# Three edits in the start-up of a fused Sinkhorn attention and expert-layer kernel: order of a sort step, width of warm-up matmuls, parts of a weight load

## The chip, the cores and the metric

One core of a Trainium2 chip runs the whole kernel. The metric is the device time of one execution in microseconds, the median of three runs. The core has five engines that run their own instruction queues and meet at semaphores: TensorE (PE; its weight loads are shown as PEld), VectorE (DVE), ScalarE (ACT), GpSimd (POOL) and SyncE (SP). Transfers are issued from the queues of GpSimd (those that change the type from f32 to f16) and SyncE, and are carried out by 16 DMA engines.

## The reference

Two parts follow each other. The attention part has q, k and v of shape (4 batches, 8 heads, 768 tokens, 64) and an 8 x 8 matrix `sort_net` for each batch and head; the expert part has 3072 tokens of width 512, four experts, and hidden width 1024:

```python
P = sort_net
for _ in range(5):
    P = np.exp(P - np.max(P, axis=-1, keepdims=True))
    P = P / (np.sum(P, axis=-1, keepdims=True) + 1e-09)
    P = P / (np.sum(P, axis=-2, keepdims=True) + 1e-09)
k_sorted = np.einsum('bhij,bhjcd->bhicd', P, k_b)   # 8 blocks of 96 tokens are mixed
v_sorted = np.einsum('bhij,bhjcd->bhicd', P, v_b)
# each block of 96 queries attends to its own block of sorted keys and values
...
p = domain_probs / (domain_probs.sum(-1, keepdims=True) + 1e-09)
for e in range(E):
    out += p[:, e:e + 1] * (np.maximum(x @ w1[e], 0.0) @ w2[e])
```

The scores are scaled by 1/8 and normalized by a softmax over the 96 keys of the block.

## The kernel before

All order is written out by hand: each engine executes its instructions in the order of the program text, and the tile framework adds the semaphore waits. Matrix operands are f16, sums are f32 in PSUM. PSUM is split into two rings of two buffers each: `psM` (taken by `psm`) and `psA` (taken by `psa`). A buffer is written again only when its readers are done.

Batch 0 is treated apart, since everything waits for it at the start. Its stages are:

- Loads. SyncE issues `sort_net` and the expert weights' probabilities. GpSimd issues, in this order, the first half of the queries (two transfers), k and v of the first four heads ("quad 0"), k and v of quad 1, and expert 0's first matrix `w1sb[0]` in two transfers (`load_w1(0, 2)`, line 173): rows 0 to 255 of the 512 (chunks `kc` 0 and 1 of 128 rows), then rows 256 to 511, each with all 1024 columns. Then it builds masks, an identity and constants.
- Warm-up. `warm(84)` (line 280) issues 84 matmuls of a constant 128 x 128 tile `dummy` with itself; their result is not used. In the last of the five sort iterations two calls of `h_q` transpose the queries on TensorE, and `warm(30)` (line 288) follows.
- Sort iterations. Five rounds of exp (ScalarE), two sums, two reciprocals and two products (VectorE) on 32 x 64 values. The last product, repeated over 16 columns into f16 (`sn16`, line 304), is split: VectorE makes rows 0 to 3 of the 8, GpSimd rows 4 to 7.
- Transposing the sort matrices. `r_half(a)` transposes one half of `sn16` with four matmuls into `Rv[:, a]`, which lies in one `psM` buffer (`ps_R`). `r_half(0)` runs at once; VectorE builds `PI0[0]` from it, the mixing operands of the lower four blocks.
- Mixing and attention. `mix_half(nm, qd, hf, pool)` mixes k or v of a quad into half `hf` of the sorted blocks with 24 matmuls, of 64 columns each; `mixed` copies two or four of the blocks out of PSUM. `h_s` makes scores with 8 matmuls and takes their exp on ScalarE; `h_w` transposes the sorted values and copies them out; `h_a` multiplies scores with values; `h_x` transposes the result into `xTs[0]`, the input of the experts.
- Expert 0's first layer, interleaved with the rest of the attention: `group0(qq, nq, g, kcs)` multiplies four chunks of 128 columns of `w1sb[0]` (group `g`: columns 0 to 511 or 512 to 1023) by the tokens, for the row chunks `kcs`. The first two calls, `group0(0, 1, 0, [0, 1])` and `group0(0, 1, 1, [0, 1])`, read rows 0 to 255, the next two rows 256 to 511.

In the order around the change, TensorE does `mix_half("k", 0, 0)`, `mix_half("v", 0, 0)`, `h_s(0, 0)`, `r_half(1)`, the transposes of `h_w`, `mix_half("k", 1, 0)`, `h_a(0, 0)`. VectorE copies both halves of `Rv` into `Rs` (f16, line 1372) after `r_half(1)`; `mix_half("k", 1, 0)` takes the `psM` buffer of `ps_R`, and so waits for that copy. `Rs` is read by GpSimd, for `PI0[1]` and for the operands of later batches. After that copy GpSimd issues the second half of the queries and expert 0's second matrix (`load_w2(0, 2)`).

Behind this start the kernel is a long row of matmuls: the experts' two layers for twelve groups of 256 tokens, most of them by a seven-product (Strassen-like) scheme, with the attention of batches 1 to 3 interleaved by the lists `PLANS`.

Of the kernel before, what the change touches and what calls it, by code (L numbers as in the profile page):

```python
# [17 lines left out]
def kernel(  # L18
# [11 lines left out]
    nc = tc.nc  # L30
# [8 lines left out]
    P = 128  # L39
# [10 lines left out]
    KH = NFC // 2  # L50
# [16 lines left out]
    def psa(shape, dtype, name):  # L67
        state["n"] += 1
        return psA.tile(shape, dtype, tag="ps", name=name)
# [36 lines left out]
    def load_natural(b, nm, qd):  # L106
        src = {"k": k, "v": v}[nm]
        t = arena[:, ds(("k", "v").index(nm) * 2 * NW + qd * NW, NW)].rearrange("p (h r d) -> p h r d", h=4, r=R)
        natural[(b, nm, qd)] = t
        nc.gpsimd.dma_start(  # L110
            t.rearrange("p h r d -> p h (r d)"),
            src[b, ds(4 * qd, 4)].rearrange("h (p r) d -> p h (r d)", r=R),
        )
# [12 lines left out]
    w1sb, w2sb = [], []  # L126
# [4 lines left out]
    def load_w1(e, parts=1):  # L131
        n = NKC // parts
        for i in range(parts):
            nc.gpsimd.dma_start(
                w1sb[e][:, ds(i * n, n)], moe_w1[e].rearrange("(kc p) f -> p kc f", p=P)[:, ds(i * n, n)]
            )
# [8 lines left out]
    def load_half_queries(hf):  # L145
        for qd in range(2):
            nc.gpsimd.dma_start(
                q0[ds(64 * qd, 64), hf].rearrange("p h r d -> p h (r d)"), half_queries(qd, hf)
            )

    dummy = Hflat[:, ds(2 * NFC * 2 * P, P)]
# [18 lines left out]
    load_natural(0, "v", 0)  # L170
    load_natural(0, "k", 1)
    load_natural(0, "v", 1)
    load_w1(0, 2)

    eye16 = const.tile([P, CP], F16, name="eye16")
    maskk = const.tile([P, P], F16, name="maskk")
# [52 lines left out]
    def spread_weights():  # L229

        nc.vector.tensor_reduce(p_den, p_in, AX.X, ALU.add)
        yield
        nc.vector.tensor_scalar(out=p_den, in0=p_den, scalar1=1e-9, scalar2=None, op0=ALU.add)
        yield
        nc.vector.reciprocal(p_den, p_den)
        yield
        nc.vector.tensor_tensor(
            p_out.rearrange("p e t -> p t e"), p_in, p_den.broadcast_to([P, NT, E]), ALU.mult
        )
        p_rows = p_dram.rearrange("e (p t) -> p e t", t=NT)  # L240
        nc.sync.dma_start(p_rows[0:S_P], p_out[0:S_P])
        nc.sync.dma_start(p_0, p_dram[0, 0:S].rearrange("(t p) -> t p", p=P))
        pbs[(0, 0)] = load_p(0, 0)
        nc.sync.dma_start(p_rows[S_P:P], p_out[S_P:P])
        yield
# [10 lines left out]
    def warm(n):  # L256
        ps = psM.tile([P, 4, P], F32, tag="ps", name=f"ps_w_{state['n']}")
        state["n"] += 1
        for m in range(n):
            nc.tensor.matmul(ps[:, m % 4, :], dummy, dummy, start=True, stop=True)  # L260

    qT0 = [from_spare(2 * S).rearrange("p (s f r x) -> p s f r x", s=2, f=2, r=R) for _ in range(2)]

    def h_q(qd, hf, copy):

        ps = psa([P, 2, R, 64], F16, f"ps_q_{qd}_{hf}")
        rows = ds(64 * qd, 64)
        for sg in range(2):
            for r in range(R):
                for hh in range(2):  # L270
                    nc.tensor.transpose(
                        ps[ds(D * hh, D), sg, r, :], q0[rows, hf, 2 * sg + hh, r, :], ident[rows, rows]
                    )
        copy(qT0[qd][:, :, hf], ps[:])
# [2 lines left out]
    srow = const.tile([GH, NB, 1], F32, name="srow")  # L277
    scol = const.tile([GH, NB, 1], F32, name="scol")
    sn16 = const.tile([GH, NB, NB, CP], F16, name="sn16")
    warm(84)  # L280
    p_steps = spread_weights()
    nc.gpsimd.tensor_copy(ident6, ident[0:R, 0:R])
    for it in range(5):
        nc.scalar.activation(sn[:], sn[:], AF.Exp, bias=0.0, scale=1.0)
        if it == 4:
            for qd in range(2):
                h_q(qd, 0, nc.scalar.copy)
            warm(30)
        nc.vector.tensor_reduce(srow[:], sn[:], AX.X, ALU.add)
        nc.vector.reciprocal(srow[:], srow[:])  # L290
        nc.vector.tensor_tensor(sn[:], sn[:], srow[:].broadcast_to([GH, NB, NB]), ALU.mult)
        nc.vector.tensor_reduce(scol[:], sn[:].rearrange("p i j -> p j i"), AX.X, ALU.add)
        nc.vector.reciprocal(scol[:], scol[:])
        if it < 4:
            nc.vector.tensor_tensor(
                sn[:], sn[:],
                scol[:].rearrange("p j o -> p o j").broadcast_to([GH, NB, NB]),
                ALU.mult,
            )
            if it:  # L300
                next(p_steps)
# [10 lines left out]
    Rv = ps_R[:, :, 0:HB * GH].rearrange("p a (i g) -> p a i g", g=GH)  # L312

    def r_half(a):
        for i in range(HB):
            nc.tensor.matmul(
                Rv[:, a, i, :], sn16[:, a * HB + i, :, :].rearrange("g j c -> g (j c)"),
                ident[0:GH, 0:GH], start=True, stop=True,
            )
# [4 lines left out]
    Rs = const.tile([P, GH, NB], F16, name="Rs")  # L324
# [31 lines left out]
    vec, act = nc.vector.tensor_copy, nc.scalar.copy  # L356
# [128 lines left out]
    def mix_half(nm, qd, hf, pool, warm_up=0):  # L485

        ps = pool([P, 1024], F32, f"ps_m{nm}_{qd}_{hf}")
        keep_warm(ps[:, 0:P], warm_up)
        tails[(nm, qd, hf)] = ps[:, 2 * R * 64:1024].bitcast(F16).rearrange("p (n x) -> p n x", n=2)
        ps = ps[:, 0:2 * R * 64].rearrange("p (s r x) -> p s r x", s=2, r=R)  # L490
        for sg in range(2):
            for r in range(R):
                for hh in range(2):
                    h = 4 * qd + 2 * sg + hh
                    nc.tensor.matmul(  # L495
                        ps[ds(D * hh, D), sg, r, :],
                        head(0, nm, h)[:, r, :],
                        PI0[hf][:, h, :, :].rearrange("p i c -> p (i c)"),
                        start=True, stop=True,
                    )  # L500
        return ps

    def mixed(nm, qd, ps, i0, n, copy):

        dst = kTs[qd][:, 0:S] if nm == "k" else vT0[qd]
        copy(
            dst.rearrange("p (i x c) -> p x i c", i=HB, c=CP)[:, :, ds(i0, n)],
            ps.rearrange("p s r (i c) -> p (s r) i c", c=CP)[:, :, ds(i0, n)],
        )
# [30 lines left out]
    def h_s(qd, qq, ps=None):  # L540

        kT, ET = kTs[qd], ETs[2 * qd + qq % 2]
        if ps is None:
            ps = psa([P, 2, 512], F32, f"ps_s0_{qd}_{qq}")
        for n in range(4):
            for hh in range(2):
                sg, i = n // 2, 2 * (qq % 2) + n % 2

                m = BLK if 2 * i + sg == 3 else P
                nc.tensor.matmul(  # L550
                    ps[0:m, hh, ds(n * BLK, BLK)],
                    kT[ds(D * hh, D), ds((2 * i + sg) * BLK, m)],
                    qT0[qd][ds(D * hh, D), sg, qq // 2, :, ds((2 * (qq % 2) + n % 2) * CP, CP)],
                    start=True, stop=True,
                )
        nc.scalar.activation(
            ET[:, 0:S].rearrange("c (h x) -> c h x", h=2), ps[0:BLK, :, 0:HS],
            AF.Exp, bias=0.0, scale=SCALE,
        )
# [806 lines left out]
    mixed("k", 0, mk0, 0, 2, act)  # L1366
    mv0 = mix_half("v", 0, 0, psa)
    mixed("v", 0, mv0, 0, 2, vec)
    h_s(0, 0)
    r_half(1)  # L1370
    mixed("k", 0, mk0, 2, 2, act)
    vec(Rs.rearrange("p g (a i) -> p a g i", a=2), Rv.rearrange("p a i g -> p a g i"))
    load_half_queries(1)
    load_w2(0, 2)
    build_PI0(nc.gpsimd, 1, 0, H, Rs[:, 0:H, HB:NB])
# [160 lines left out]
```

## Time and profile before

| What | Value |
|---|---|
| Time, median of 3 runs | 359.16 us (359.14 to 359.62) |
| Profiled execution: span from first to last instruction | 357.8 us (its time around the span is not listed apart) |
| Instructions | 9498, of them 3949 matmuls and 3949 weight loads |
| TensorE busy | 351.6 us, 98% of the span |
| VectorE, ScalarE, GpSimd busy | 276.2, 170.6, 133.6 us |
| Granted TensorE clock | 1.00 in all slices |
| DMA share in the first 40 us | above 0.9 of the engines from about 3 us on |

In the rows of the timeline a line reads: start in us, duration in us of the merged group, engine, source line, operation, names written and read, shapes, count, and in brackets the idle time of the engine just before and what ended it; "issue" there means that the profile shows nothing that the engine waited for. In the table of windows each engine's entry is its busy time in the window and, in brackets, the number of its instructions. A matmul's duration includes its way through the array, so that matmuls issued 0.03 us apart show 0.2 us each and overlap.

### The profile page before, as it was taken

The page shows a single profiled execution, that of the slowest core. Times are in us where ns is not written, and L with a number is a line of the kernel's source. Part 1 is how long each engine was busy: PE and PEld are TensorE (multiplying, and loading weights), DVE is VectorE, ACT ScalarE, POOL GpSimd, SP SyncE. Part 2 cuts the span into 40 slices and gives each one's busy share as a digit, 9 for nine tenths or more (in the row PEclk, how much of TensorE's full clock was granted, in tenths as well). Part 3 has the DMA queues.
Part 4 walks back from the last instruction along what each step waited for, and adds up shares of the span by engine and source line. Part 5 has one row for each costly group of instructions (what it writes and reads, how often), then busy time and mean ns, then how long its engine had stood idle before and what let it go on. Part 6 is the DMA issues. An engine that isn't in the chain of part 4 may idle for free.

```text
span 357.8 us, 9498 instructions
## 1 busy us (share of the span) xinstructions
PE 351.6 (98%) x3949; PEld 306.3 (86%) x3949; DVE 276.2 (77%) x552; ACT 170.6 (48%) x303; POOL 133.6 (37%) x149
## 2 busy tenths in 40 slices
PE   8899999999999999999999999999999999999996
PEld 8686867888888888888899988888888888888886
DVE  5754797869889587868978988896678886588963
ACT  2554240442434535367947258830288611688201
POOL 8864010375122222000535318840058800188400
PEclk9999999999999999999999999999999999999999
DMA  8999999999999999935996420005200015100011
GB/s 114 207 205 228 216 210 198 209 163 165 201 154 160 188 152 170 194 74 73 168 201 90 102 78 0 2 2 108 102 29 2 3 39 138 61 0 2 2 73 46
DMA packets 72022, 40.51 MB, mean 113 GB/s; under 512 B 40614, under 2 KB 66732, under 8 KB 71980
## 3 DMA queue, kind: packets, MB, share of 16 engines
q0 software_dynamic: 36576, 19.93, 41.9%
q1 hardware_dynamic: 35260, 19.92, 28.5%
q8 instruction: 31, 0.51, 0.6%
q14 instruction: 11, 0.09, 0.1%
q10 hardware_dynamic: 144, 0.07, 0.1%
HBM read 42.13 MB, written 6.34 MB: 135 GB/s over the span
## 4 chain that ended last, share of the span: by engine, by line
PE 95%; DVE 2%; ACT 1%; DMA 0%; issue 0%; DVEq 0%
PE ps_h L790 18%; PE ps_Q L1264 18%; PE ps_p L774 12%; PE ps_X L1121 10%; PE ps_Z L1121 7%; PE ps_Q L1121 7%; PE ps_Z L1264 6%; PE ps_h L679 3%; PE ps_o L714 3%; PE ps_p L830 3%; PE ps_a L453 2%; PE ps_s L418 2%; PE ps_k L399 1%; PE ps_v L365 1%; PE ps_a L567 1%; PE ps_mk L495 1%
## 5 line engine op out<-in xcount | busy, mean ns | idle before, releaser
L790 PE MATMUL ps_h<-xT,w 128*128 128x256 f16 x576 | 67.5, 273 | 0.0
L790 PEld LDWEIGHTS <-w 128*128 128x128 f16 x576 | 55.2, 98 | 7.2
L796 DVE SCALAR_TENSOR_TENSOR Hb<-ps_h,pb 128x1024 f16<-128x1024 f32 x34 | 41.5, 1223 | 17.2 <-PE ps_h L790 15.8
L1121 PEld LDWEIGHTS <-w 128*128 128x128 f16 x480 | 43.6, 98 | 4.8
L1134 POOL TENSOR_TENSOR arena<-tmp,pb 128x512 f16<-128x512 f32 x12 | 15.2, 1275 | 65.7 <-PE ps_Z L1121 49.8
L1264 PEld LDWEIGHTS <-Hb 128*128 128x128 f16 x320 | 31.1, 98 | 3.5
L1133 ACT ACTIVATE tmp<-tmp 128x512 f32<-128x512 f32 x46 | 29.0, 632 | 3.9 <-DVE tmp L1171 3.9
L1264 PEld LDWEIGHTS <-Sb 128*128 128x128 f16 x304 | 28.3, 98 | 3.0
L1121 PEld LDWEIGHTS <-arena 128*128 128x128 f16 x312 | 27.7, 98 | 2.9
L425 ACT ACTIVATE ET<-ps_s 96x768 f16<-96x768 f32 x24 | 18.0, 802 | 25.1 <-PE ps_s L418 24.8
L121 POOL DMA_DIRECT2D arena<-in_q_dram x24 | 19.9, 838 | 25.5 <-DMA q_ring<-arena 25.2
L408 ACT CAST kT<-ps_k 64x384 f16<-64x384 f32 x48 | 22.7, 473 | 13.3 <-PE ps_k L399 12.3
L1121 PE MATMUL ps_X<-ET,arena 128*128 128x256 f16 x168 | 25.2, 272 | 0.0
L1264 PE MATMUL ps_Q<-w,Hb 128*128 128x256 f16 x192 | 24.6, 273 | 0.0
L774 PEld LDWEIGHTS <-Hb 128*128 128x128 f16 x232 | 21.8, 98 | 3.0
L1127 DVE SCALAR_TENSOR_TENSOR Hb<-ps_X,pb 128x512 f16<-128x512 f32 x27 | 18.7, 691 | 7.0 <-PE ps_X L1121 7.0
L1141 ACT COPY ps_X<-ps_Z 128x512 f32<-128x512 f32 x27 | 15.4, 571 | 17.8 <-PE ps_Z L1121 17.8
L1121 PE MATMUL ps_Z<-xT,w 128*128 128x256 f16 (+1 forms) x176 | 22.5, 258 | 0.0
L760 DVE TENSOR_TENSOR Sb<-Hb 128x512 f16<-128x512 f16 x33 | 20.6, 647 | 0.0
L1148 ACT COPY tmp<-ps_X 128x512 f32<-128x512 f32 x26 | 15.2, 585 | 9.2 <-PE ps_X L1121 6.6
L1127 DVE SCALAR_TENSOR_TENSOR Hb<-ps_Z,pb 128x512 f16<-128x512 f32 x27 | 18.4, 682 | 1.3 <-PE ps_Z L1121 1.3
L1171 DVE TENSOR_TENSOR tmp<-ps_Q,tmp 128x512 f32<-128x512 f32 x26 | 17.8, 683 | 0.8 <-PE ps_Q L1121 0.8
(266 smaller groups left out, 741.6 us busy)
## 6 DMA issues: line engine op xcount, KB each, us to landing
w<-in_moe_w_dram POOLq DMA_DIRECT2D x6, 1024.0 KB, 27.9
pb<-p_dram SPq DMA_DIRECT2D x9, 512.0 KB, 7.0
arena<-in_k_dram POOLq DMA_DIRECT2D x8, 384.0 KB, 9.3
arena<-in_v_dram POOLq DMA_DIRECT2D x8, 384.0 KB, 7.5
vs<-arena SPq DMA_DIRECT2D x36, 66.0 KB, 4.9
arena<-in_q_dram POOLq DMA_DIRECT2D x24, 96.0 KB, 7.5
out_dram<-ob SPq DMA_DIRECT2D x9, 256.0 KB, 2.0
w<-in_moe_w_dram POOLq DMA_DIRECT2D x4, 512.0 KB, 12.5
```

What stands on the lines that cost most here:

```text
L121: nc.gpsimd.dma_start(t[:, h // 2, :, h % 2, :], q[b, h].rearrange("(t p) d -> p t d", p=P))
L408: nc.scalar.copy(kT[ds(D * hh, D), r], pk[ds(D * r, D), hh].rearrange("p a (i c) -> p a i c", c=CP),)
L425: nc.scalar.activation(ETs[2 * (pr % 2) + hh][:, 0:S].rearrange("c (a x) -> c a x", a=2), pss[hh][0:BLK, :, 0:HS], AF.Exp, bias=0.0, scale ...
L760: tt(sm[0], blk(0, 1), blk(1, 1), ALU.add)
L774: nc.tensor.matmul(ps, lhs(e, f), Ts[e][rhs][:, f, :], start=(first and e == es[0] and f == 0), stop=(done and e == es[-1] and f == KH - 1 ...
L790: nc.tensor.matmul(ps[:, f, :], w1sb[e][:, kc, ds((4 * g + f) * P, P)], xT[:, kc, ds(2 * c * P, 2 * P)], start=(kc == 0), stop=(kc == NKC ...
L796: nc.vector.scalar_tensor_tensor(out=Hb[:, homes.get(e, e), ds(4 * g, 4), :], in0=ps[:], scalar=0.0, op0=ALU.max, in1=weights(e).broadcast ...
L1121: nc.tensor.matmul(dst[:, ds(f * cols, cols)], a[lhs][:, k, ds((f0 + f) * P, P)], t[rhs][:, k, :], start=(first and f == 0 and k == 0), st ...
L1127: nc.vector.scalar_tensor_tensor(out=home(i, j), in0=src.rearrange("p (f x) -> p f x", f=m), scalar=0.0, op0=ALU.max, in1=weight(j).broadc ...
L1133: nc.scalar.activation(src, src, AF.Relu, bias=0.0, scale=1.0)
L1171: tt(t12, Q, u2, ALU.add)
L1264: nc.tensor.matmul(ps, lhs(e, f), Ts[e][rhs][:, f, part], start=(first and e == 0 and f == 0), stop=(e == E - 1 and f == KH - 1), skip_gro ...
```

## The change

Three edits:

1. `load_w1(0, 2)` is replaced by four transfers: rows 0 to 255 with columns 0 to 511, the same rows with columns 512 to 1023, then rows 256 to 511 in the same two halves. Each moves half of what one transfer moved before.
2. `warm(n)` issues matmuls whose moving operand is `dummy` repeated four times, 512 columns into a whole PSUM bank, in place of 128 columns. The calls go from `warm(84)` to `warm(21)` and from `warm(30)` to `warm(8)`.
3. `r_half(1)` and the copy of `Rv` into `Rs` move ahead of `h_s(0, 0)`; the copy is made by ScalarE (`act`) and no longer by VectorE (`vec`).

```diff
-    load_w1(0, 2)
+    for i in range(2):
+        for j in range(2):
+            nc.gpsimd.dma_start(
+                w1sb[0][:, ds(2 * i, 2), ds(KH * P * j, KH * P)],
+                moe_w1[0].rearrange("(kc p) f -> p kc f", p=P)[:, ds(2 * i, 2), ds(KH * P * j, KH * P)],
+            )
...
         for m in range(n):
-            nc.tensor.matmul(ps[:, m % 4, :], dummy, dummy, start=True, stop=True)
+            nc.tensor.matmul(
+                ps[:], dummy, dummy.rearrange("p (o x) -> p o x", o=1).broadcast_to([P, 4, P]), start=True, stop=True
+            )
...
-    warm(84)
+    warm(21)
...
-            warm(30)
+            warm(8)
...
     mixed("v", 0, mv0, 0, 2, vec)
+    r_half(1)
+    act(Rs.rearrange("p g (a i) -> p a g i", a=2), Rv.rearrange("p a i g -> p a g i"))
     h_s(0, 0)
-    r_half(1)
     mixed("k", 0, mk0, 2, 2, act)
-    vec(Rs.rearrange("p g (a i) -> p a g i", a=2), Rv.rearrange("p a i g -> p a g i"))
     load_half_queries(1)
     load_w2(0, 2)
     build_PI0(nc.gpsimd, 1, 0, H, Rs[:, 0:H, HB:NB])
```

`KH * P` is 512. In the text below, `mix "k",1` stands for `mix_half("k", 1, 0)`.

## The prediction

> **What bounds the kernel now.** I read the page's shares first, then the chain that ended last, then the first 37 us by windows, then TensorE's timeline there, and last the DMA answers for single packets.
>
> ```profile
> PE 351.6 (98%) x3949; PEld 306.3 (86%) x3949; DVE 276.2 (77%) x552; ACT 170.6 (48%) x303; POOL 133.6 (37%) x149
> ...
> q8 instruction: 31, 0.51, 0.6%
> ...
> PE 95%; DVE 2%; ACT 1%; DMA 0%; issue 0%; DVEq 0%
> ```
>
> TensorE is the bound: 351.6 us busy of a 357.8 us span, 95% of the chain. What is left is the start. The windows (PE, PEld, DVE, ACT, POOL busy, clock, DMA) show where:
>
> ```profile
> 11.70:14.00 2.30, 1.97 (x61) 1.65 (x62) 1.16 (x4) 0.48 (x1) 2.30 (x4) 1.00 1.31 206
> 14.00:17.00 3.00, 2.67 (x75) 2.24 (x76) 2.29 (x6) 2.19 (x5) 3.00 (x4) 1.00 1.14 212
> 17.00:20.50 3.50, 3.09 (x69) 2.64 (x62) 2.47 (x7) 2.27 (x4) 2.18 (x5) 1.00 1.18 205
> 20.50:37.00 16.50, 16.50 (x296) 11.94 (x293) 8.35 (x17) 8.49 (x12) 8.98 (x10) 1.00 1.18 221
> ```
>
> From 20.5 us on TensorE never stops (16.50 of 16.50), so a head start won before 20.5 us goes through to the end. Before 11.79 us the sort iterations on VectorE and ScalarE set the time; the change does not touch them. Everything is decided between 11.79 and 20.5 us, a chain of hops between TensorE, ScalarE and VectorE. Its rows on TensorE:
>
> ```profile
> 1.06 7.20 PE L260 MATMUL ps_w<-Hb 128*128 128x128 f16 x84 [1.06 <-DVE Hb L152]
> 8.19 0.85 PE L271 MATMUL ps_q<-ident,T 64*64 64x64 f16 x48
> 8.97 1.85 PE L260 MATMUL ps_w<-Hb 128*128 128x128 f16 x30
> 11.79 0.26 PE L316 MATMUL ps_R<-ident,sn 32*128 32x32 f16 x4 [0.98 <-DVE sn L304]
> ...
> 13.78 0.21 PE L550 MATMUL ps_s<-Sb,kT 64*128 64x96 f16 x1 [0.19 <-ACT kT L506]
> 14.17 0.33 PE L550 MATMUL ps_s<-Sb,kT 64*128 64x96 f16 x7 [0.18 <-issue]
> 14.44 0.26 PE L316 MATMUL ps_R<-ident,sn 32*128 32x32 f16 x4
> 14.62 0.42 PE L522 MATMUL ps_mv<-ident,Sb 128*96 128x128 f16 x4
> 15.21 0.57 PE L495 MATMUL ps_mk<-Sb,arena 128*64 128x64 f16 x24 [0.16 <-DVE Rs L1372]
> ...
> 20.27 0.37 PE L522 MATMUL ps_s<-ident,Sb 128*96 128x128 f16 x3 [0.20 <-issue]
> ```
>
> Two of these stops wait for nothing in the program ("issue"): after the first matmul of h_s(0,0), and after the first transpose at 19.85. Counting matmuls and their weight loads in the timeline, they are exactly 256 instructions apart, and the page's queue q8 moved 31 packets of 16 KB for 2 x 3949 = 7898 TensorE instructions, 255 each. So the stops are ends of instruction blocks. A DMA window of 0.02 us holds one such packet:
>
> ```profile
> q8 instruction: 1, 0.02, 295.3%
> ```
>
> 295.3% of 16 engines for 0.02 us is 0.94 us: the packet lies at 11.79 to 12.73, and the stop ends 1.44 us later. The next lies at 17.86 to 18.80, and its stop ends 1.47 us later, at 20.27. Each packet starts 3.6 to 3.7 us after the stop before it ends. A block thus comes 3.65 + 0.95 + 1.45 = 6.05 us after it is asked for, and between 8 and 20 us TensorE's short matmuls eat 256 instructions about that fast. The start is partly bound by instruction fetch.
>
> **Warm-up matmuls (84 to 21, 30 to 8).** Same columns (84 x 128 = 21 x 512), 32 x 128 in place of 30 x 128. The old ones pace at 5.0 us / 47 = 106 ns until 6 us and 2.2 / 40 = 55 ns after; 128x512 matmuls elsewhere (L714, four in 1.04 us at 379 ns each) are 0.22 us apart. So 21 wide ones take about 5.0 + 9.3 x 0.22 = 7.05 us against 7.20, and 8 take 8 x 0.22 + 0.16 = 1.9 against 1.85: no time, under the sort iterations, which release TensorE at 11.79 either way. If that cover (0.98 us) were gone they would still cost within 0.1. What counts is that 85 matmuls and 85 weight loads are gone: block ends move 170 instructions later in the work. The stop at 14.17 costs 14.17 - 13.78, less one 0.02 us step, 0.37 us; the stop at 20.27 costs 0.20 on TensorE but only about 0.05 beyond what VectorE allows there (its xsl op ends at 20.32, and the next matmuls wait for it).
>
> The Trainium skill's page "Runtime: NRT & Kernel Launch", section "Instruction fetch mechanics", has the same 16 KiB blocks of 256 instructions but calls the cost of crossing "one DMA tail-bump, mostly hidden". By that rule this edit would bring nothing; these two rows say 0.37 and 0.20, and the rows decide.
>
> The Trainium skill's page "TensorE: Matmul & The Clock Gate", Part 1, speaks against fewer, idler warm-ups: an idle window of about 3.4 us halves the clock. The idle stretch before 11.79 stays near one microsecond, so by that rule nothing happens.
>
> **r_half(1) and the copy of Rs.** r_half(1) is four matmuls 0.03 us apart. It moves into the 0.19 us hole in which TensorE waits for ScalarE's kT copy (13.25 + 0.48): 0 to 0.1 us on the path, I take 0. Its input from GpSimd ends at 12.65, 12.9 with the later issues below, before 13.6. The copy costs VectorE 0.42 now; on ScalarE, where 384 columns take 0.48 and 768 take 0.81, 256 columns make about 0.37, at 13.9 to 14.3, inside ScalarE's 0.81 us of idle time before its exp. Behind that wait stand the exp and the second kT copy, neither later than now. If the cover were gone it would cost its 0.37.
>
> Step by step, before to after: h_s(0,0) finishes at 14.12 and not 14.50 (its twin at 16.45 takes 0.34 without a stop). The exp runs 14.25 to 15.05, before to 15.35. The transposes of h_w at 14.62 wait only for VectorE's copy (13.63 + 0.56 = 14.19): 14.24, gain 0.38. VectorE's evacuation (15.15) follows: 14.77, gain 0.38. mix "k",1 no longer waits for Rs: 14.62 and not 15.21, gain 0.59, but its readers are not first in line. The second transposes wait for VectorE's next copy (ends 16.04, then 15.66): gain 0.38. That is carried through 16.72, 17.34, 17.95 and 18.95; the vanished second stop adds 0.05. Sum: 0.43 us ahead at 20.5.
>
> **Expert 0's first matrix in four.** GpSimd issues four transfers of about 0.73 us where it issued two (1.43): 1.45 more, of which 1.22 lie in its idle time before L304. Its half of the sort matrices, the queries and w2 behind it are issued some 0.23 us later. The trace shows that an issue waits for the landing of the eighth one before it (w2's at 21.46 right after w1's second half landed at 6.97 + 14.2 = 21.2), so some later issues wait up to 1.7 us for quarters; the queue holds over 10 us of work then, so it does not run dry. Rows become 1 KB packets: windows of those run at 206 GB/s against 211 with 2 KB, 0.1 us on 1 MB. Benefit: the two halves landed at 18.05 and 21.2 and are first read at 19.16 and 21.67. With the 0.43 us head start the second would be read at 21.24, with nothing to spare; as quarters the rows needed there land near 20. So this part gains nothing by itself and keeps the rest. Bounds: 0.3 lost, 0.1 gained; I take 0. Later transfers keep 1.3 us or more (the weights pb land at 38.3, read at 39.6).
>
> **Sum.** The profiled span is 357.8; the median of the runs, 359.16, is 1.3 us more, lying around the span and unchanged. 359.16 - 0.43 = 358.73; I take off little for the fetch (below): 358.8. A measurement of this kernel tells about 0.2%, 0.7 us, from no change.
>
> **Rivals.**
> 1. The fetch wait moves instead of going (slower than forecast, to slower than before). In the new stream the block ends fall at instruction 13 of mix "k",0, in h_x(0,[0]) (now 17.22, then 16.85), and in work now at 24.7 and 30.2. The block needed at 16.85 is asked for when the sequencer passes the first of these. TensorE waits from 10.7 to 11.79 with that point 37 instructions ahead. If the sequencer runs that far ahead, it asks by 10.5 or earlier, and the block is there by 16.6; if it runs only some 25 ahead, as the packet at 11.79 taken back 3.65 us suggests, it asks at 12.0, the block comes at 18.05, and 1.2 us are lost: 0.8 slower, 359.9. For running far ahead: the packet at 198.60 starts 1.67 us, 31 instructions, before TensorE gets to its block end, with its own delay still to be added. A smaller form: 256 instructions between 24.7 and 30.2 take 5.5 us, below the 6.05, so 0 to 0.4 may be lost there. It decides from a request later than 10.8 us. Place: 359.2 to 360.1. Chance 0.23.
> 2. More comes than the sum: the 0.59 of mix "k",1 and both stops in full (0.59 + 0.20) go through, because ScalarE's kT copies and not VectorE's were last: 358.3, range 358.0 to 358.5. Against it: VectorE's rows follow each other without a gap from 15.15. Chance 0.19.
> 3. The change does not do what it says: stops are a fixed price per block end and land elsewhere on the path, leaving only Rs: about 0.1 to 0.2, 359.0. Against it: block ends at 26.8 and 33.1 show no stop. Chance 0.10.
>
> The forecast itself (358.4 to 359.1) has 0.48.
>
> **Numbers.** Faster by over 0.2% (under 358.44): rival 2 nearly whole (0.17) and the forecast's edge (0.07), 0.24. Slower (over 359.88): 0.15, the upper part of rival 1 with a DMA wait taken in. Within: 0.61. The range 358.1 to 360.0 leaves out about 0.08 below and 0.10 above.
>
> **What would show it.** Right: no "issue" gap near 14 and 20 us; Rs on ScalarE at 13.9; mix "k",1 near 14.6 with no wait on Rs; the first ps_h (L679) group near 18.8; later rows some 0.4 us earlier. Wrong: an "issue" gap of a microsecond in h_x near 17, a wait of L679 on a transfer of w, or half-speed matmuls after 11.8.

## The result

The change is slower: 361.27 us median of 22 runs (360.25 to 365.56) against 359.62 for 22 runs of the kernel before on the same chip (359.14 to 361.97). The ratio is 1.0054, 95% interval 1.0038 to 1.007. The forecast was 358.8 with a range of 358.1 to 360.0. The kernel before itself came out 0.46 above the median of three runs (359.16) from which the forecast started.

The page after (shares, instruction queues, the chain that ended last):

```profile
PE 351.1 (97%) x3864; PEld 300.6 (83%) x3864; DVE 276.1 (77%) x551; ACT 170.9 (47%) x304; POOL 135.1 (37%) x151
...
q8 instruction: 30, 0.49, 0.6%
q14 instruction: 12, 0.10, 0.1%
...
PE 91%; DVE 3%; DMA 3%; ACT 1%; SPq 1%; issue 1%; DVEq 0%
```

TensorE has 85 matmuls and 85 weight loads fewer and one instruction block fewer (30 packets on q8, before 31), but its share of the chain fell from 95% to 91%. ScalarE's busy instructions went from 303 to 304, VectorE's from 552 to 551.

TensorE's timeline (start, duration, engine, line of the changed kernel, operation, operands, count, idle time before and its cause), after:

```profile
1.06 6.26 PE L265 MATMUL ps_w<-Hb 128*128 128x512 f16 x21 [1.06 <-DVE Hb L152]
...
8.03 1.90 PE L265 MATMUL ps_w<-Hb 128*128 128x512 f16 x8
11.89 0.26 PE L323 MATMUL ps_R<-ident,sn 32*128 32x32 f16 x4 [1.96 <-DVE sn L311]
...
13.88 0.35 PE L557 MATMUL ps_s<-Sb,kT 64*128 64x96 f16 x8
14.34 0.42 PE L529 MATMUL ps_mv<-ident,Sb 128*96 128x128 f16 x4
14.69 0.57 PE L502 MATMUL ps_mk<-Sb,arena 128*64 128x64 f16 x24
...
16.93 0.26 PE L605 MATMUL ps_a<-perm,xsl 96*128 96x96 f16 x2
17.71 0.25 PE L605 MATMUL ps_a<-perm,xsl 96*128 96x96 f16 x2 [0.52 <-issue]
...
19.49 0.82 PE L686 MATMUL ps_h<-xT,w 128*128 128x192 f16 x8
```

Up to 16.93 us everything is within about 0.1 us of the forecast: the stop in h_s is gone, h_w stands at 14.34 (before 14.62), mix "k",1 at 14.69 without a wait on Rs (before 15.21). Then the stop is back, in h_x, and the first ps_h group comes at 19.49 and not at 18.8; before it came at 19.19. The stop stands exactly 256 matmuls and weight loads behind the block end of 12.83 us (mix "k",0). (A block is 256 instructions, which one 16 KB packet on queue q8 brings; a block end is the place where TensorE goes over from one block to the next.) The packet that this stop waits for starts at 15.52, as the DMA view of the 0.02 us from there on shows:

```profile
q8 instruction: 1, 0.02, 304.4%
```

The windows (PE, PEld, DVE, ACT, POOL busy, clock, DMA) after; the first rows are those shown for before:

```profile
11.70:14.00 2.30, 2.07 (x70) 1.84 (x72) 1.16 (x4) 0.56 (x2) 2.30 (x4) 1.00 1.31 203
14.00:17.00 3.00, 2.75 (x82) 2.20 (x79) 2.05 (x5) 2.65 (x6) 2.11 (x4) 1.00 1.26 206
17.00:20.50 3.50, 2.90 (x49) 2.37 (x48) 2.08 (x5) 1.99 (x4) 2.47 (x5) 1.00 1.25 203
20.50:37.00 16.50, 16.36 (x293) 11.99 (x293) 8.28 (x18) 8.49 (x12) 9.89 (x12) 1.00 1.19 220
140.00:190.00 50.00, 47.98 (x595) 41.72 (x593) 38.88 (x79) 28.84 (x46) 7.81 (x7) 1.00 0.72 137
```

TensorE is busier than before up to 17 us (2.07 and 2.75 against 1.97 and 2.67) and less from there to 20.5 (2.90 against 3.09). The last row is a second place: 2.0 us lost between 140 and 190, where the kernel before was full (50.00 of 50.00). The waits of TensorE name them:

```profile
PE ps_a L460 <- DMA vs<-arena: 1.3, 1, 1.3
PE ps_s L425 <- ACT arena L378: 0.7, 1, 0.7
```

The third place is the end. The last output is issued by SyncE 2.8 us before the span's end in the kernel before (355.01 of 357.8) and 3.2 us before it after (357.58 of 360.8). The DMA views from the last matmul on, before and then after (issue, KB, us to landing):

```profile
q14 instruction: 1, 0.01, 0.9%
...
out_dram<-oa SPq DMA_DIRECT2D x1, 64.0 KB, 1.6
```

```profile
q14 instruction: 1, 0.01, 1.0%
...
out_dram<-oa SPq DMA_DIRECT2D x1, 64.0 KB, 2.0
```

Both have one 8 KB packet of instructions there, but in the kernel before it starts 3.71 us after the last matmul, when the span is over (3.19), and after the change 1.06 us after it, while the output is under way.

The profiled run after took 362.56: 3.0 us more span than before's profile, of which 0.2 are left of the start at 37 us (a row stands at 37.85, before 37.65), some 2.4 come at the two late waits (TensorE's rows are 0.2 behind before's at 155 us, 1.1 at 173 and 2.6 at 188), and some 0.4 from the tail (the stretch from the last matmul to the end of the span). It is one of the slower runs; the lowest run, 360.25, is 1.1 above before's 359.14.

### The profile page after: what moved, and what is told of

It is laid out like the page before. It is cut to its first block, busy times and chain, and to the rows that moved or that the text cites. A ratio compares the mean times of both kernels' runs of the same rounds, so it can differ in the third digit from the quotient of the medians.

```text
span 360.8 us, 9330 instructions
## 1 busy us (share of the span) xinstructions
PE 351.1 (97%) x3864; PEld 300.6 (83%) x3864; DVE 276.1 (77%) x551; ACT 170.9 (47%) x304; POOL 135.1 (37%) x151
## 4 chain that ended last, share of the span: by engine, by line
PE 91%; DVE 3%; DMA 3%; ACT 1%; SPq 1%; issue 1%; DVEq 0%
PE ps_h L797 18%; PE ps_Q L1271 17%; PE ps_X L1128 10%; PE ps_p L781 10%; PE ps_Z L1128 7%; PE ps_Q L1128 7%; PE ps_Z L1271 6%; PE ps_o L721 3%; PE ps_h L686 3%; PE ps_p L837 3%; DMA vs<-arena 2%; PE ps_a L460 1%; PE ps_s L425 1%; PE ps_k L406 1%; PE ps_v L372 1%; SPq L386 1%
```

## The experiments

Diffs are against the kernel before unless said, in e4 against the changed kernel. Medians of before in the four batches: 359.49 (e1 to e4), 359.49 (e5 to e8), 359.53 (e9 to e12), 359.36 (e13, e14).

**Each edit alone, and one mend.** e1: the wide warm-ups alone (edit 2). e2: the four-part load alone (edit 1). e3: the move of r_half(1) and Rs alone (edit 3). e4: the whole change with its first warm-up cut finer:

```diff
-    warm(21)        # 512 columns each
+    warm(42, 2)     # 256 columns each
```

> The kernel before with the wide warm-up matmuls alone (21 and 8 of 512 columns). Theory 1 (two causes: the end of an instruction block moves into h_x near 17 us and costs the start 0.1 to 0.5 us; the rest of the slow-down comes from the two more issues on GpSimd's queue): a stop marked issue of 0.3 to 0.7 us inside h_x near 17.5 us, none at 14.2 and 20.3 us, the first ps_h group of expert 0 at 19.3 to 19.8 us (19.19 before), no stop of TensorE between 155 and 185 us, and a time 0.1 to 0.5 us above the kernel before. Theory 2 (the fetch of instructions is the whole cause, the later stops follow from any shift of the start): the same start, stops between 155 and 185 us as well, and 1 to 2 us above the kernel before. Theory 3 (four transfers alone are the cause): the kernel before within 0.2 us.

> The kernel before with expert 0's first matrix loaded in four transfers, and nothing else. Theory 1: the start as before (stops at 14.2 and 20.3 us, first ps_h group at 19.2 us), stops of TensorE of together about 1 us or more between 155 and 185 us for the copies of the sorted values (vs), and a time 0.7 to 1.5 us above the kernel before. Theory 2: the kernel before within 0.3 us. Theory 3: 1 to 2 us above.

> The kernel before with r_half(1) and the copy of Rs ahead of h_s(0,0), the copy on ScalarE, and nothing else. All theories: the stop at an instruction block's end stays inside h_s(0,0) or moves by the 8 instructions of r_half(1), mix k,1 no longer waits for Rs, the first ps_h group comes 0.1 to 0.3 us sooner than 19.19 us, and the time is 0 to 0.3 us below the kernel before. If any shift of the start brings the later stops (theory 2), it can be up to 1 us above.

> The changed kernel with the first warm-up as 42 matmuls of 256 columns in place of 21 of 512: 42 more instructions, so that the first block end falls into the second warm-up and its follower is asked for some 3 us sooner. Theory 1: no issue stop in h_x, first ps_h group at 18.7 to 18.9 us, 0.6 to 0.8 us sooner than in the changed kernel; the later stops between 155 and 185 us stay, and the time is 0.4 to 0.9 us below the changed kernel (0.5 to 1 us above the kernel before). Theory 2: the later stops go too, and the time is about 0.4 us below the kernel before. Theory 3: the changed kernel within 0.2 us.

| Kernel | Median | Lowest | Ratio (95%) |
|---|---|---|---|
| e1 wide warm-ups | 360.86 | 360.09 | 1.0044 (1.0029 to 1.006) |
| e2 four-part load | 359.5 | 359.13 | 0.9993 (0.998 to 1.0005) |
| e3 Rs moved | 360.09 | 359.53 | 1.001 (0.9996 to 1.0024) |
| e4 whole, 42 x 256 | 360.24 | 359.72 | 1.0027 (1.0011 to 1.0042) |

Edit 2 is most of the loss, edit 1 nothing. e1's timeline has the stop at the same instruction, longer, and the clock goes after it (two rows of the timeline, then windows with PE and clock):

```profile
18.27 0.24 PE L600 MATMUL ps_a<-perm,xsl 96*128 96x96 f16 x2 [1.15 <-issue]
...
20.18 0.67 PE L681 MATMUL ps_h<-xT,w 128*128 128x192 f16 x3
```

```profile
17.00:20.50 3.50, 2.26 (x39) 0.91 1.18 203
19.90:23.30 3.40, 3.40 (x31) 0.50 1.27 206
```

From 19.89 to 23.3 us TensorE ran at half clock, so that one stop was paid twice in that run. In e4 21 more matmuls put the first block end at 9.51 us in place of 12.8, and the stop is gone: first ps_h at 18.82. Yet the median of e4 stays 0.75 above before, and that of e3 0.6 (e3's interval takes in no change), although both reach ps_h earlier than before's profile. Something else seems to cost, in edit 3. e3's own profile shows one place:

```profile
31.03 0.22 PE L249 MATMUL ps_o<-T 6*128 6x6 f32 x1 [0.45 <-DMA T<-p_dram]
```

TensorE is there 0.4 early and waits for the weights p, which go to DRAM and back from 20 us on.

**Count, look-ahead and the trip of p.** e5: edits 1 and 3 with the old warm-ups. e6: the whole change with the second warm-up as `warm(16, 2)` for `warm(8)`, 16 instructions more between the first block end and the wait on sn. e7: e5 with the last step of p earlier. e8: the kernel before with that alone:

```diff
     h_a(1, 0, ps_a10)   # e7, e8
-    next(p_steps)
...
+    next(p_steps)
     even01 = h_a(0, 1, ps_s01, True)
```

> The change without its wide warm-ups: four-part load, r_half(1) early, Rs on ScalarE, warm-ups 84 and 30 matmuls of 128 columns as before. Theory F (the loss is one instruction-block wait that fewer warm-up instructions move into h_x): the block ends fall as in the kernel before, no issue stop over 0.3 us in h_x near 17 us, no fall of the granted clock near 20 us, and a median 0.8 to 1.4 us under the change's 361.27, that is 359.9 to 360.4. Theory S (moving Rs to ScalarE costs by itself): it stays near 360.7 to 361.3. Theory T (the head start is stopped at about 31 us by the read of the first weights p from DRAM, L249, whose landing is set by a DMA round trip that begins on VectorE at 20 us): TensorE is 0.3 to 0.4 ahead of the kernel before at 19 us, and a wait of L249's line on T of 0.2 to 0.6 us near 31 us takes most of it back.

> The whole change, its second warm-up as 16 matmuls of 256 columns in place of 8 of 512: the same columns, 16 more instruction pairs by count (8 matmuls and 8 weight loads). The first block end after the warm-ups is then 21 instructions behind the point where TensorE waits for sn, and not 37. Theory F with a sequencer that runs 25 to 35 instructions ahead: the block is asked for before the wait, at about 10 us, its packet comes near 13.5 and not 15.5, the stop in h_x is gone, and the median is 0.8 to 1.2 us under the change's 361.27 (360.1 to 360.5). A stop of fixed price at each block end: the stop stays and stands 16 instructions earlier, 361.2. Wide matmuls slow by themselves: 361.2 too, without a stop in h_x.

> The four-part load and the move of r_half(1) and Rs with narrow warm-ups, and the last step of the spread of p (one 128x96 product on VectorE, then the DMA write of p and its read back) placed ahead of h_a(0,1) and not behind h_a(1,0). Theory T: the write is issued near 18.9 us and not 20.2, T is read back near 29.5, L249's line has no wait, the 0.4 us of head start stay, and it is 0.3 to 0.6 faster than the same kernel without this move: 359.3 to 359.7, under the kernel before if that stands at 359.5. Rival (the head start is lost later, in waits for transfers of vs and xT between 150 and 185 us, or was never there): no gain over the kernel without the move.

> The kernel before with that earlier step of p alone. Theory T: the kernel before comes to L249's line at 31.0 us, about when T lands, so nothing or at most 0.1 to 0.2 us is won: 359.3 to 359.5. Rival (p's read back binds the kernel before as well in most runs): 0.3 to 0.5 us faster.

| Kernel | Median | Lowest | Ratio (95%) |
|---|---|---|---|
| e5 edits 1 and 3 | 360.22 | 359.47 | 1.0029 (1.0011 to 1.0047) |
| e6 whole, 16 ahead | 361.64 | 361.15 | 1.006 (1.0045 to 1.0075) |
| e7 e5, p earlier | 359.84 | 359.57 | 1.0015 (1.0 to 1.0029) |
| e8 p earlier alone | 359.44 | 359.14 | 0.9999 (0.9988 to 1.0009) |

e6 speaks against the look-ahead idea: with the block end 21 instructions behind the waiting one, and not 37, the packet still does not come as if it had been asked for during the wait. TensorE goes on at 11.84 and passes the block end at 12.37, the packet comes at 15.60, and the stop stands at the same instruction number, which is now in the mixing of v:

```profile
17.98 0.28 PE L503 MATMUL ps_mv<-Sb,arena 128*64 128x64 f16 x6 [1.12 <-issue]
```

e5 has no stop in h_x and no wait on p, and is still 0.7 over before. e8, whose TensorE stream is before's, has no stop in h_s, and its first ps_h comes at 18.82, exactly where e5 and e4 have it:

```profile
13.79 0.35 PE L550 MATMUL ps_s<-Sb,kT 64*128 64x96 f16 x8 [0.19 <-ACT kT L506]
...
14.26 0.42 PE L522 MATMUL ps_mv<-ident,Sb 128*96 128x128 f16 x4
```

So in a run without the stop the early sort matrices win nothing: 18.82 with and without edit 3. And e7's profile has a stop at the same instruction number as before's, although it has edit 3 and the old count, and a half clock behind it (0.54 in the window 17.00 to 20.50):

```profile
14.71 0.22 PE L321 MATMUL ps_R<-ident,sn 32*128 32x32 f16 x3 [0.99 <-issue]
```

The stop comes and goes from run to run. Where a block end is passed (by counting 256 instructions back from the stop), where the next packet starts and where TensorE goes on at the next block end, in us:

| Profile | First end passed | Packet | Next end | Stop | First ps_h |
|---|---|---|---|---|---|
| e5 | 7.97 | 11.06 | 13.57 | none | 18.82 |
| before | 8.37 | 11.79 | 14.17 | 0.39 | 19.19 |
| e8 | 8.62 | 11.36 | 13.79 | none | 18.82 |
| e7 | 8.63 | 12.36 | 14.71 | 1.16 | 20.64 |
| e4 | 9.51 | 12.31 | 16.44 | none | 18.82 |
| e6 | 12.37 | 15.60 | 17.98 | 1.32 | 20.16 |
| e1 | 12.74 | 15.87 | 18.27 | 1.36 | 20.18 |
| after | 12.83 | 15.52 | 17.71 | 0.72 | 19.49 |

(Stops here are from start to start of TensorE's instructions, so they are 0.2 more than the idle time in the rows.) A packet starts 2.7 to 3.7 us after the end before it is passed, and where TensorE waits, it goes on 2.2 to 2.4 us after the packet's start. That makes 4.9 to 6.1 us from one end to the release of the next (up to 6.4 in e13, further down), and fits each row: the old count passes the first end near 8 us and needs the next block at 13.4 to 13.8, so it stops in some runs (in 4 of the 11 profiles with the old count: before, e7, e12 by 0.35 and e13 by 0.24); the new count passes it at 12.4 to 12.8, behind the wait on sn, and needs the next some 4.2 us later, so all three profiles of that kind stop; e4 has 6.9 us and does not.

**The tail, and shape against count.** The tail after the last matmul is 3.15 to 3.2 us in the profiles of before, e1, e2 and e8, and 3.5 to 3.8 in e3 to e7 and after: it is long in all six that copy Rs with ScalarE, in none of the others. e9 tests it with one more ScalarE instruction, e10 is e7 with six, e11 is e4 with the earlier p and six, e12 keeps the matmul count and changes only the shapes:

```diff
+            nc.scalar.copy(pad[:], dummy[:, 0:1])   # e9: once; e10, e11, e14: six times; e13: twice
...
-    warm(84)
+    warm(84, 12)    # e12, e14: 12 of 512 columns, 72 of 64
-            warm(30)
+            warm(30, 4)
```

> The kernel before with one instruction more on ScalarE: a copy of 128x1 at about 10 us, where ScalarE is idle. Theory E (moving the Rs copy to ScalarE adds one instruction to ScalarE's stream, its last instruction block then ends 2.7 us earlier, and the fetch of the next one, an 8 KB packet, falls on the landing of the last output): the 8 KB packet comes about 1.1 us after the last matmul and not 3.7, the tail from the last matmul to the end of the span grows from about 3.14 to 3.5 us, and the whole is 0.4 us slower: 359.8 to 360.0, the fastest runs near 359.5 in place of 359.15. Rival (the tail is set by something else that came with the move): no packet there, 359.5, fastest 359.15.

> Four-part load, r_half(1) early, Rs on ScalarE, narrow warm-ups, the earlier step of p, and six 128x1 copies more on ScalarE at about 10 us, so that ScalarE's block end moves away from the tail. Theory E: no 8 KB packet between the last matmul and the last output's landing, tail back at 3.1 us, 0.4 us under the same kernel without the copies (359.84): 359.3 to 359.6. Theory that the kernel before has nothing left to win at its start (its usual run has no issue stop at 14 us, the stop was one of the profiled run): not under 359.2 at the median. Rival (the move of Rs gains 0.3 to 0.4 at the start, hidden so far by the tail): 359.0 to 359.2, the fastest under 358.9.

> The whole change with its first warm-up as 42 matmuls of 256 columns, the earlier step of p and the six copies on ScalarE. Block ends at 9.5, 16.4 and 23.3 us: 6.9 us apart, over the 5 to 6 us that a block takes from the crossing of one end to its release, so no issue stop even where the clock opens late. Theory E with this: 0.4 under 360.24, 359.5 to 359.8, the fastest near 359.3. Rival (wide matmuls cost by their shape): 360.2 still.

> The kernel before with wide matmuls in its warm-ups at unchanged instruction counts: of 84, 12 of 512 columns and 72 of 64; of 30, 4 of 512 and 26 of 64. About the same columns as before. Theory F (count, not shape): block ends as in the kernel before, no stop in h_x near 17 us, 359.3 to 359.8. Theory W (the shape of the warm-ups, by the clock or by power): the clock falls near 20 us or the time is 0.8 to 1.5 us above before, as with the wide ones alone (360.86).

| Kernel | Median | Lowest | Ratio (95%) |
|---|---|---|---|
| e9 one more on ScalarE | 359.67 | 359.24 | 1.0007 (0.9997 to 1.0017) |
| e10 e7, six more | 359.44 | 359.12 | 1.0003 (0.9985 to 1.0021) |
| e11 e4, p earlier, six more | 359.94 | 359.31 | 1.0008 (0.9996 to 1.0021) |
| e12 wide, old count | 359.57 | 359.08 | 1.0001 (0.9988 to 1.0014) |

e12 against e1 settles the warm-ups: wide matmuls cost nothing at the old count of instructions (1.0001) and 1.0044 at the lower one. e10 has no instruction packet behind the last matmul, and its last output lands as in the kernel before:

```profile
q10 hardware_dynamic: 144, 0.07, 5.8%
issues: line engine op xcount, KB each, median us to landing
out_dram<-oa SPq DMA_DIRECT2D x1, 64.0 KB, 1.6
```

It is 0.40 under e7 by the medians and 0.45 by the lowest runs, as forecast, though the two intervals overlap. e11 is 0.3 to 0.4 under e4, in the same way; its profiled run (360.41) lost 0.5 us in a wait of ps_s on ScalarE at 162 us and 0.4 in one on VectorE at 98 us. e9 missed: the packet came 3.59 us after the last matmul and the tail was 3.29, with ScalarE standing 0.4 us in the closing barrier. The move of Rs adds two entries to ScalarE's stream and not one, the copy and a semaphore wait ahead of it (in e5 at 13.83 and 13.27). So the last batch:

> The kernel before with two 128x1 copies more on ScalarE at about 10 us. Theory E, mended (the move of Rs adds two entries to ScalarE's stream, the copy and a semaphore wait, and with one entry the block end still lay in the final barrier): the 8 KB packet comes about 1.1 us after the last matmul, the last output lands 0.4 us later, the tail is 3.5 us in place of 3.14, the median 0.35 to 0.45 over before, the fastest runs near 359.55. Rival (the tail is from something else in the move): packet near 3.6 to 3.7, fastest 359.15 to 359.25.

> The whole change, its warm-ups at the old number of matmuls (12 of 512 columns and 72 of 64; 4 of 512 and 26 of 64) and six 128x1 copies more on ScalarE. If the two block ends are all that the change loses: no stop in h_x near 17 us, tail 3.14, and the time of before, 359.3 to 359.7, fastest near 359.15. If something else in it costs (ScalarE's copy, the four issues on GpSimd): 359.8 or more. If the early sort matrices win 0.2 to 0.4 of themselves: 359.0 to 359.3 at the median.

| Kernel | Median | Lowest | Ratio (95%) |
|---|---|---|---|
| e13 two more on ScalarE | 360.07 | 359.47 | 1.0017 (1.0008 to 1.0026) |
| e14 whole, both counts mended | 359.75 | 359.13 | 1.0005 (0.9994 to 1.0017) |

e13, which does two useless 128x1 copies at 10 us and nothing else, has the packet 1.07 us after the last matmul, a tail of 3.47 in place of 3.19, and a loss: 0.38 us by the lowest runs, 0.6 by the ratio. That the packet is ScalarE's is seen from how it moves with ScalarE's entries alone: 3.71 us after the last matmul before, 3.59 with one more (e9), 1.07 with two. Its view from the last matmul on:

```profile
q14 instruction: 1, 0.01, 0.9%
issues: line engine op xcount, KB each, median us to landing
out_dram<-oa SPq DMA_DIRECT2D x1, 64.0 KB, 1.9
```

e14 brings the whole change back to before within what can be told (1.0005, interval 0.9994 to 1.0017). No version beats the kernel before.

## Why the prediction was wrong

**The gain that was summed (0.43) belongs to some runs only.** The step "the median of the runs, 359.16, is 1.3 us more, lying around the span" is wrong. In every run for which both are known, of all kernels, the time is 1.73 to 1.92 us over the span. So a span of 357.8 was a run of about 359.6, the slowest of the three shown (359.62): the sum took a stop of a slower run off the time of a faster one. Six profiles have before's order and count of TensorE's instructions at that place. Three have the stop (before 0.39, e12 0.35, e13 0.24 us), and three do not (e2, e8, e9); e2 and e8 reach the first ps_h at 18.86 and 18.82, before's profile at 19.19. The chain of steps held in the profile after (h_s 13.88, h_w 14.34, mix "k",1 14.69), but a run of the kernel before without the stop does as well. How many of its runs stop is not known; at the median no gain shows. e10, with edits 1 and 3 and no loss in the tail, is at 359.44 against 359.53 and its lowest run at 359.12 against 359.14, and e14's interval, from 0.9994 on, leaves no room for 0.43. That mix "k",1 is 0.15 earlier without the wait on Rs (14.69, in e8 14.84) is on no path, as forecast.

**The stop moved: rival 1.** Place and mechanism are as written: instruction 13 of mix "k",0, then h_x. The failed step is the look-ahead, on which the forecast rested that no stop is left. It was argued that the sequencer, while TensorE waits from 10.7 to 11.79, stands some 37 instructions further, past the block end, and so has asked by 10.5. It had not: the packets came at 15.52, and at 15.60 in e6 with only 21 instructions to go. Less the prediction's 3.65 us from request to packet, that is a request at 11.9, the moment at which sn released TensorE (11.89 and 11.84); less the 2.7 us that the table has at least, it is at the passing of the block end itself. The sequencer acts as if it does not run past an instruction that waits for a semaphore, be the block end 37 or 21 instructions away; the packet at 198.60, which spoke for running ahead, lies in a stretch in which TensorE does not stand still. The profile shows packets and not requests, so an early request that is held back would look the same; but in these three profiles (after, e6, e1) the packet follows the passing of the end by 2.7 to 3.2 us, no later than with the old count (2.7 to 3.9). The rival's 1.2 us are what e1 and e6 lost (1.36 and 1.32); the profile after lost 0.72. Against a run without a stop the first ps_h is 0.67 late (19.49 against 18.82). Chance given: 0.23; the forecast had the other branch.

**Rs on ScalarE, "0 on the path".** True at the start: ScalarE copies at 13.92 and its exp follows at 14.27, where 14.25 was forecast. But the two entries move ScalarE's own block end from the closing barrier to just ahead of the last output, and the fetch that follows falls on that output's landing: the tail is 0.36 us longer in the profile after, 0.28 in e13, which adds two entries and nothing else, and not longer in e10 (3.14), where six more entries move the block end away. No rival had it; the prediction counted TensorE's blocks only. 0.67 and 0.36 make 1.03, which is close to the distance of the lowest runs (360.25 and 359.14, 1.11). The rest of the medians' distance, some 0.6, is not accounted for one by one: longer stops, as e1 and e6 show, are part of it, and so are late waits (below) and stretches at half clock. Five of the 22 runs after have a mean granted clock of 0.986 to 0.995, among them the slowest (365.56); of the 120 runs of the kernel before in the four batches one is that low. e1's profile, with one stretch of 3.4 us at half clock, has 0.995.

**"A head start won before 20.5 us goes through to the end."** Not in e3, where the wait for p took 0.45 back (e12's profile waits 0.8 us there, without a head start). In e7 and e10 no such wait is left. In the profile after 2.4 us came on top later, in a wait of the scores (ps_s) at 162.57 for ScalarE's copy of ps_v, and in one for vs at 181.73. By the program that copy overwrites what six transfers `vs`, issued by SyncE just before, read. The issue of the last of them, before and then after, with the DMA view of 0.02 us from 157.65 on:

```profile
157.41 0.60 SPq L379 DMA_DIRECT2D vs<-arena  x1
...
157.62 1.92 SPq L386 DMA_DIRECT2D vs<-arena  x1
...
q8 instruction: 1, 0.02, 472.8%
```

A packet of TensorE's instructions starts beside the long issue. In all five profiles with fewer warm-up instructions (after, e1, e4, e6, e11) one of these six issues takes 1.2 to 1.9 us and a 16 KB packet starts within 0.1 us of it; in the eleven with the old count no packet starts there and none of the six takes over 0.61. The wait on ScalarE's copy follows in four of the five (after 0.7, e1 0.4, e6 0.3, e11 0.5, not e4) and in none with the old count. The wait for vs has the same sign in the profile after: an issue at 173.44 takes 1.77 us (before 1.07), with a packet at 173.49. So the shifted blocks go with these waits too; no run moves one such packet alone, so this is read from the profiles and not tested.

**Warm-ups "no time".** Right for the columns: 6.26 and 1.90 us for 21 and 8 matmuls, forecast 7.05 and 1.9 (the spacing of the wide matmuls fell from 0.43 to 0.22 us already at some 4.3 us in this run), and e12 shows it. "The idle stretch before 11.79 stays near one microsecond" was wrong by as much, 1.96, and harmless: the granted clock held, there and in e4 (1.49). It fell behind the stops instead: in e1 after 1.15 us of idle time and in e7 after 0.99. The Trainium skill's page "TensorE: Matmul & The Clock Gate", Part 1, which was weighed before, asks for an idle window of some 3.4 us. The half clock did last 3.4 us (19.89 to 23.3 in e1), but neither run had an idle stretch near that length, so an unbroken idle stretch is not the condition here.

**The four-part load, 0.** Right: e2 at 0.9993. **The range** ended at 360.0 because the moved stop was priced against a median that was taken to contain the old one, because ScalarE's block had no price, and because 359.16, the median of three runs, stood in for 359.62.

The Trainium skill's page "Runtime: NRT & Kernel Launch", section "Instruction fetch mechanics", calls the cost of crossing a block end "mostly hidden". Here it is not: e1 against e12 (1.0044 and 1.0001) prices it on TensorE, e13 (1.0017) on ScalarE.

## What to carry to other kernels

Count instructions as a resource of each engine: an edit that adds or drops them moves every later block end of that engine, and here the cost was decided by where the ends landed, on a stretch of short matmuls or on the last output. Keep the counts when only shapes are to change. With the DMA engines as full as here, block ends that TensorE reaches 5 to 6 us apart stopped it in some profiles and not in others; 6.8 and 6.9 us (e11, e4) were free. Before a stop of a profile is put into a sum, ask which run was profiled: span plus the fixed rest must give the time that the gain is taken from.

## What the runs showed that was not expected

- A TensorE block of 256 instructions is there only 4.9 to 6.4 us after the end before it is passed, while the DMA engines are full, and in three profiles its packet came no sooner although TensorE waited on a semaphore 21 or 37 instructions ahead of that end. With the same TensorE instructions, e8 passes the second end after 5.2 us without a stop, and before's profile waits until 5.8.
- Two 128x1 copies on ScalarE at 10 us cost about 0.4 us at 356 us: with an 8 KB packet of instructions beside the last output it lands after 1.9 to 2.0 us in place of 1.6.
- Between 154 and 160 us a transfer's issue on SyncE took 1.2 to 1.9 us in place of 0.6 when a packet of TensorE's instructions started beside it, in five profiles of five. It is no strict rule: in e1 an issue at 84.93 took 0.59 with such a packet at 84.99.
- A stop of 0.7 us or more amid short matmuls was followed by 3.4 us at half clock in two of the four profiles that have one (e1, e7; not after, not e6). What decides it is open.
